# A recurrent state kernel with a feed-forward stage: all chunks read in 1,280-byte runs, state products in 64x64 quarters, weights loaded by casting transfers

## The chip, the core and the metric

The kernel runs on one core of a Trainium2 chip. The core has a matrix engine (TensorE, PE in the profile, with its weight loads listed as PEld), three elementwise engines (VectorE as DVE, ScalarE as ACT, GpSimd as POOL), a sequencer that mostly issues transfers (SyncE, SP), and 16 DMA engines. The engines run side by side and wait for each other through semaphores. The metric is the device time of one execution in microseconds, as the median of several runs.

## The reference

There are 4 batches of 8 heads, so 32 independent recurrences, over 768 steps with 40 features. Each keeps a 40 x 40 state. The output of all heads, put side by side (320 features for each of 3,072 tokens), goes through a feed-forward stage.

```
state = 0                                   # per batch and head, 40 x 40
for t in range(768):
    y[t]  = r[t] @ state
    Sa    = state @ a[t]
    state = state * w[t][None, :] - outer(Sa, b[t]) + outer(v[t], k[t])
x = y, heads side by side                   # 3072 x 320
out = square(max(x @ w_in, 0)) @ w_out      # w_in 320 x 2048, w_out 2048 x 320
```

All inputs and the output are float32 in HBM.

## The kernel before

**Chunks.** The 768 steps are cut into 12 chunks of 64. Inside a chunk the recurrence is written as matrix products; only the state passes from chunk to chunk. For each chunk the kernel takes the logarithm of w (`ln`), splits it into two bfloat16 parts (`hi`, `lo`), and sums them over the steps with triangular matmuls: `cf` gives the sums turned (features by steps), `ci` gives them straight (steps by features). Their exponentials scale a and r (decay up to a step) and k and b (its inverse).

**Turning.** The products need some operands turned, which TensorE does as transpositions: `TA`, `TR` (a and r), `TK` (k and b), `BK` (k and b turned, scaled and turned back), `TV` (v and the corrections), `TS` (the state), `XT` (the output). Each writes PSUM, and an elementwise engine copies or multiplies it out under the same name in small letters (`tA`, `tR`, `tK`, `bK`, `tV`, `tS`, `xt`). Chunks in `WHOLE` (0 to 3, function `tmode`) turn 128 x 128 at a time; later ones turn two halves of 64 rows each. A few turns go by DMA (`dK`, `dV`, `dS`).

**The products of a chunk**, for all 32 heads:
- `EN`, `CX`: the triangular matrices within the chunk, masked on DVE (`mEN`, `mCX`).
- `AS`: a against the old state; `EV`: the triangular matrix against v; `u0`, `NU`, `u1`: one correction step. Together they give the rows that update the state.
- `SC`, `S`, `s`: the new state (old state carried over, plus k and b against v and the corrections; then scaled and stored by DVE at line 808).
- `RS`, `Y`, `y`, `yd`: the output from the old state and from within the chunk.
- `F`, `FL`, `f`, `q`, `O`, `o`, `st`: the feed-forward stage of the chunk's 256 tokens: input matmuls (`F` over 256 features, `FL` over the last 64), max with 0, square, output matmuls, copy and store.

**Loading.** `load(c)` issues the six inputs of a chunk from SP, two transfers each. Where rows go by steps, a run is one head's 40 features, 160 bytes; where a partition holds eight steps, a run is 8 x 40 x 4 = 1,280 bytes. a and r use the 1,280-byte form in every chunk; k and b use it in chunks in `RUNS` (0 to 2; `turned_kb`, line 501), and the 160-byte form otherwise; w and v use 160 bytes. k and b of chunks outside `RUNS` are scaled straight (`mulKB`) and then turned. The weights come from SP as float32 into buffers used later for other things (lines 1040, 1048, 1062) and are cast by an elementwise engine (`cwl`, `cwi`, `cwo`).

**What sets the order.** The kernel lists every operation once with its reads and writes (`plan.add`), and the text `ORDER` says in which order and on which engine each is issued; `PE0` to `PE3` name the PSUM slot that a group takes. A slot is free again when the engine that empties it is done. Each engine executes its own list strictly in order, so an instruction that waits holds everything behind it on that engine. Matmuls are issued at line 402, half-row transpositions at 406 and 128 x 128 ones at 409. `rows(g)` is the lower or upper half of the 128 partitions.

**Tile shapes.** `pe(name, mode, ...)` names the array shape of a group: D is the whole 128 x 128 array, R two row halves, C two column halves, Q quarters of 64 x 64. In the kernel before, AS, RS, SC, S and Y are C; EV is C in chunks 3 to 11, for which the unused half of VU is zeroed (`zu`); NU is Q.

Of the kernel before, what the change touches and what calls it, by code (L numbers as in the profile page):

```python
# [86 lines left out]
ORDER = """SP ldw 0; SP ldb 0; SP ldk 0; POOL zv 1; POOL zr 0; SP ldk 1; ACT ln 0; SP ldb 1; POOL hi 0; ACT  # L87
castB 0; POOL zr 1; DVE lo 0; SP ldw 1; DVE castK 0; PE0 cf 0; DVE zs 0; PE1 TK 0; DVE zk 0; ACT
eg 0; SP lda 0; PE2 ci 0; POOL castB 1; DVE tK 0 g0; SP ldr 0; DVE zv 0; DVE castK 1; SP ldv 0;
ACT ln 1; ACT hi 1; POOL castA 0; ACT ef 0; SP lda 1; DVE lo 1; PE3 TA 0; ACT exw 0; DVE tK 0 g1;  # L90
SP ldw 2; PE0 cf 1; DVE tA 0 g0; ACT ef 1; DVE tA 0 g1; PE1 EN 0 g0; POOL castV 0 g1; PE2 TK 1;
DVE zk 2; SP ldb 2; ACT eg 1; DVE mEN 0 g0; POOL castV 0 g0; PE3 BK 0; POOL castA 1; SP ldk 2; DVE
tK 1 g0; POOL castR 0; POOL zv 2; DVE tK 1 g1; SP lda 2; PE1 EN 0 g1; POOL zk 1; PE0 ci 1; DVE mEN
0 g1; PE2 TA 1; ACT exw 1; SP ldr 1; ACT ln 2; DVE bK 0; PE0 EV 0; SP ldv 1; POOL castB 2; PE1 BK
1; DVE hi 2; ACT u0 0; DVE tA 1 g1; POOL lo 2; DVE bK 1; PE3 EN 1 g1; PE NU 0; DVE tA 1 g0; POOL
zs 1; ACT u1 0 g0; SP lwi 0 k1 x1; DVE mEN 1 g1; PE1 EN 1 g0; ACT u1 0 g1; PE2 S 0 g0; SP lwi 0 k1
x2; DVE mEN 1 g0; SP ldw 3; ACT castK 2; POOL castA 2; PE3 TR 0; PE S 0 g1; ACT tRw 0; PE0 cf 2;
DVE s 0 q1; PE1 TV 0; ACT eg 2; POOL castV 1 g1; DVE s 0 q0; SP lwi 0 k1 x3; PE3 ci 2; SP lwi 0 k1
x0; DVE tV 0; POOL zu 3 g0; ACT ef 2; SP lwo 0 x0; PE2 TA 2; POOL castV 1 g0; ACT exw 2; SP lwi 0
k0 x2; DVE tA 2 g1; PE0 CX 0 g0; POOL zu 3 g1; PE1 AS 1; ACT castR 1; SP lwi 0 k0 x1; DVE mCX 0  # L100
g0; PE EV 1; SP lwi 0 k0 x0; SP ldv 2; DVE tA 2 g0; PE0 CX 0 g1; ACT u0 1; PE3 TK 2; DVE mCX 0 g1;
ACT ln 3; PE NU 1; PE2 TR 1; ACT hi 3; POOL cwi 0 k1h0; DVE tK 2 g1; PE0 TS 0; ACT u1 1 g0; SP lwi
0 k0 x3; POOL cwi 0 k1h1; DVE tK 2 g0; ACT u1 1 g1; SP lwl 0; ACT tRw 1; POOL lo 3; PE1 Y 0; SP
ldb 3; PE3 EN 2 g1; ACT tS 0; DVE yd 0; DVE y 0; PE2 TV 1; POOL cwo 0 x0; DVE mEN 2 g1; PE1 SC 1;
ACT tV 1; PE S 1 g0; PE S 1 g1; PE0 EN 2 g0; DVE s 1 q0; PE3 XT 0; POOL castV 2 g0; DVE s 1 q1;
ACT xt 0; PE2 BK 2; SP ldr 2; DVE mEN 2 g0; POOL cwi 0 k0h0; ACT castV 2 g1; PE3 ci 3 h0; PE1 AS
2; POOL cwi 0 k0h1; ACT ei 3 h0; DVE bK 2; PE EV 2; ACT ex 3 h0 g1; PE0 ci 3 h1; ACT ex 3 h0 g0;
DVE u0 2; PE2 CX 1 g0; ACT ex 3 h1 g1; PE3 F 0 u0; SP lda 3; ACT ei 3 h1; DVE cwl 0; ACT ex 3 h1
g0; DVE mCX 1 g0; PE NU 2; PE0 F 0 u2; ACT u1 2 g0; SP lwo 0 x1; SP ldk 3; ACT u1 2 g1; PE2 CX 1
g1; PE FL 0 u2; DVE mCX 1 g1; PE FL 0 u0; PE1 FL 0 u1; ACT f 0 u0; PE F 0 u1; DVE f 0 u2; PE2 RS  # L110
1; ACT f 0 u1; PE3 SC 2; PE S 2 g0; POOL castA 3; PE S 2 g1; ACT q 0 u1; SP lwo 0 x2; PE0 FL 0 u3;
DVE s 2 q0; PE Y 1; DVE s 2 q1; PE1 cf 3; SP ldv 3; PE F 0 u3; ACT ef 3; DVE cwo 0 x1; DVE yd 1;
DVE y 1; PE3 TA 3; ACT f 0 u3; PE1 TV 2; DVE tA 3 g0; POOL mulKB 3 h1; ACT castR 2; SP lwo 0 x3;
DVE tA 3 g1; PE0 XT 1; PE2 TS 1; ACT xt 1; DVE mulKB 3 h0; PE3 TR 2; ACT tV 2; DVE tS 1; SP ldw 4;
PE0 TK 3; DVE cwo 0 x2; PE2 F 1 u2; DVE tK 3; ACT tRw 2; POOL castV 3 g1; PE1 FL 1 u1; PE FL 1 u2;
SP ldr 3; PE3 EN 3 g1; POOL castV 3 g0; ACT f 1 u2; PE0 EN 3 g0; DVE mEN 3 g1; PE F 1 u1; POOL cwo
0 x3; SP lwo 0 x4; PE2 F 1 u0; SP ldk 4; DVE mEN 3 g0; ACT f 1 u1; PE3 CX 2 g1; PE FL 1 u0; DVE
mCX 2 g1; PE1 CX 2 g0; ACT ln 4; PE0 TS 2; ACT f 1 u0; POOL hi 4; DVE mCX 2 g0; PE3 AS 3; POOL lo
4; PE EV 3; SP lwo 0 x5; PE2 RS 2; DVE tS 2; ACT u0 3; PE Y 2; POOL zu 4 g0; ACT castR 3; PE NU 3;
DVE y 2; PE0 FL 1 u3; ACT u1 3 g0; DVE yd 2; PE1 ci 4 h1; SP ldb 4; DVE cwo 0 x4; PE F 1 u3; ACT  # L120
ex 4 h1 g0; DVE q 0 u0; ACT u1 3 g1; DVE q 0 u2; PE2 TR 3; ACT ei 4 h1; PE3 SC 3; PE S 3 g0; ACT
# [6 lines left out]
ACT ln 5; PE3 FL 2 u3; SP ldr 5; PE F 2 u3; ACT o 0; DVE hi 5; DVE mEN 4 g0; ACT f 2 u0; POOL lo
5; PE2 RS 3; PE Y 3; SP ldw 6; ACT f 2 u3; PE0 FL 2 u1; DVE y 3; POOL q 1 u0; PE1 cf 5; DVE yd 3;
PE3 EN 4 g1; ACT ef 5; PE F 2 u1; DVE mEN 4 g1; SP lda 5; ACT castV 4 g0; PE2 XT 3; POOL castR 4;  # L130
PE1 F 2 u2; DVE xt 3; ACT castV 4 g1; POOL q 1 u3; DVE f 2 u1; SP ldb 5; PE FL 2 u2; PE2 ci 5 h0;
PE3 AS 4; ACT ex 5 h0 g1; DVE f 2 u2; PE EV 4; ACT ei 5 h0; POOL q 2 u3; PE0 TS 3; ACT ex 5 h0 g0;
DVE u0 4; ACT ln 6; PE2 ci 5 h1; SP ldk 5; PE1 TR 4; DVE tS 3; ACT ei 5 h1; POOL castR 5; PE NU 4;
# [18 lines left out]
DVE mCX 5 g1; POOL q 3 u3; ACT castV 6 g1; PE0 AS 6; SP ldr 6; PE2 RS 5; ACT f 4 u1; PE EV 6; POOL
mulKB 7 h1; PE Y 5; ACT u0 6; SP ldk 8; PE1 cf 7; DVE y 5; PE3 ci 7 h0; PE NU 6; DVE yd 5; POOL
castA 7; ACT ei 7 h0; PE2 O 3 u0; DVE u1 6 g0; ACT ln 8; SP ldr 7; ACT ef 7; DVE u1 6 g1; POOL
castR 6; PE O 3 u1; SP ldw 9; DVE hi 8; ACT ex 7 h0 g0; ACT ex 7 h0 g1; DVE q 3 u2; PE1 TA 7; PE0
TV 6; DVE mulKB 7 h0; PE3 TR 6; ACT tV 6; PE O 3 u2; DVE tA 7 g1; DVE lo 8; PE O 3 u3; SP ldv 7;
DVE tA 7 g0; ACT tR 6 g1; ACT tR 6 g0; PE0 TK 7; ACT o 3; PE1 XT 5; DVE tK 7; PE3 SC 6; PE S 6 g0;
# [966 lines left out]
```

## Time and profile before

| | |
|---|---|
| runs | 244.72 us median of 3 (241.68, 244.72, 244.88) |
| profiled execution | span 241.4 us from first to last instruction; the page gives no other time of it. The lowest run is 0.3 us above the span |
| TensorE | 219.8 us busy (91%), 5,360 matmuls |
| VectorE, ScalarE, GpSimd | 185.1 (77%), 171.9 (71%), 119.3 us (49%) |
| DMA | 116,808 packets, 37.20 MB, mean 154 GB/s; 103,575 packets under 512 bytes; the SP queue's packets take 75.7% of the 16 engines' span |
| mean granted TensorE clock | 0.975 of full speed |

A busy share is an average over stages with different limits, so it has to be read stage by stage. The timeline gives the start and the length of a group of matmuls; since matmuls overlap in the pipeline, the cost of a group in a full stretch is the start of the next group minus its own. An entry `[2.78 <-DMA raw_kb<-in_b_dram]` says that the engine sat idle 2.78 us before the instruction and that a transfer ended the wait.

### The profile page before, as it was taken

How to read it: one execution, taken by the hardware profiler on the slowest of the kernel's cores; microseconds unless marked ns; L12 is line 12 of the kernel's file. 1: busy time of each engine (PE TensorE's matmuls, PEld its weight loads, DVE VectorE, ACT ScalarE, POOL GpSimd, SP SyncE). 2: the span in 40 equal slices, each digit the busy share in tenths (PEclk: the TensorE clock that was granted, in tenths of full speed). 3: DMA queues.
4: the chain of work that ended last, by engine and by line, in shares of the span. 5: the costliest groups of instructions: out<-in, count | busy, mean ns of one | idle time of the engine just before them, and what ended most of it. 6: DMA issues, size and time to landing. Idle time of an engine off the chain costs nothing.

```text
span 241.4 us, 11825 instructions
## 1 busy us (share of the span) xinstructions
PE 219.8 (91%) x5360; PEld 173.8 (72%) x5360; DVE 185.1 (77%) x237; ACT 171.9 (71%) x225; POOL 119.3 (49%) x117
## 2 busy tenths in 40 slices
PE   0569877999999999999999999999999999999992
PEld 0357666778887787777777877877787777877872
DVE  3779994889988898899789978779888668646430
ACT  3383876879699888976979995975897974572330
POOL 6237816403545572849948379318591750024330
PEclk9967997999999999999999999999999999999998
DMA  6989999997979987888783878978994857093413
GB/s 154 233 185 231 186 217 162 187 203 156 181 158 236 187 163 148 144 194 152 157 169 67 168 178 161 220 157 144 146 188 120 156 106 93 3 161 72 109 24 86
DMA packets 116808, 37.20 MB, mean 154 GB/s; under 512 B 103575, under 2 KB 116375, under 8 KB 116503
## 3 DMA queue, kind: packets, MB, share of 16 engines
q1 hardware_dynamic: 115574, 36.13, 75.7%
q8 instruction: 42, 0.69, 1.2%
q10 hardware_dynamic: 1184, 0.33, 0.6%
q14 instruction: 8, 0.06, 0.1%
HBM read 28.84 MB, written 3.93 MB: 136 GB/s over the span
## 4 chain that ended last, share of the span: by engine, by line
PE 74%; DMA 8%; SPq 7%; DVE 4%; ACT 3%; issue 2%; POOL 1%; POOLq 0%; ACTq 0%
PE pb L402 65%; PE pb L406 6%; DMA G<-in_moe_w_in_dram 4%; PE pb L409 3%; DMA osb<-in_moe_w_out_dram 2%; SPq L433 2%; SPq L1048 2%; DMA raw_w<-in_w_dram 2%; SPq L425 1%; DVE AR L682 1%; POOL WIN L392 1%; SPq L465 1%; DVE VU L385 1%; ACT lnW L548 1%; ACT VU L388 1%
## 5 line engine op out<-in xcount | busy, mean ns | idle before, releaser
L402 PE MATMUL pb<-WOUT,G 128*128 128x320 bf16 (+1 forms) x400 | 57.0, 294 | 0.1
L973 POOL TENSOR_TENSOR G<-G 128x1024 bf16<-128x1024 bf16 x22 | 41.8, 1910 | 28.4 <-ACT G L965 23.4
L402 PE MATMUL pb<-XT,WIN 128*128 128x256 bf16 x384 | 48.3, 273 | 0.0
L402 PEld LDWEIGHTS <-G 128*128 128x128 bf16 x400 | 36.4, 98 | 13.8 <-issue 0.5
L965 ACT ACTIVATE G<-pb 128x1024 bf16<-128x1024 f32 x36 | 36.0, 1021 | 11.1 <-PE pb L402 9.6
L402 PEld LDWEIGHTS <-WIN 128*128 128x128 bf16 x384 | 34.7, 98 | 8.0 <-issue 3.7
L713 DVE TENSOR_TENSOR EN<-pb,MSK 128x1024 bf16<-128x1024 f32 x24 | 28.8, 1216 | 4.9 <-PE pb L402 4.8
L713 DVE TENSOR_TENSOR CX<-pb,MSKI 128x1024 bf16<-128x1024 f32 x24 | 28.7, 1218 | 3.5 <-PE pb L402 3.2
L396 POOL TENSOR_TENSOR KB<-raw_kb,iG 128x640 bf16<-128x640 f32 x10 | 15.8, 1580 | 16.7 <-ACT iG L584 14.9
L808 DVE TENSOR_TENSOR STb<-pb,GT 64x640 bf16<-64x640 f32 x22 | 18.1, 821 | 3.4 <-PE pb L402 3.0
L392 POOL CAST VU<-raw_v 64x640 bf16<-64x640 f32 x17 | 13.3, 785 | 13.3 <-DMA raw_v<-in_v_dram 12.8
L896 DVE TENSOR_TENSOR Yb<-pb,Gin 128x128 bf16<-128x128 f32 (+1 forms) x24 | 12.3, 553 | 9.5 <-PE pb L402 9.4
L590 ACT ACTIVATE Gin<-pb 64x320 f32<-64x320 f32 x36 | 15.4, 428 | 4.6 <-PE pb L402 4.2
L396 POOL TENSOR_TENSOR lo<-lnW,hi 128x640 bf16<-128x640 f32 x7 | 9.8, 1402 | 16.4 <-DVE hi L383 16.2
L402 PE MATMUL pb<-XT,WLAST 64*128 64x256 bf16 x192 | 17.1, 271 | 0.0
L682 DVE TENSOR_TENSOR AR<-pb,GT 128x512 bf16<-128x512 bf16 x24 | 15.9, 683 | 1.6 <-PE pb L406 1.4
L402 PEld LDWEIGHTS <-EN 64*64 64x64 bf16 (+1 forms) x768 | 14.5, 111 | 3.4 <-issue 2.2
L388 ACT ACTIVATE VU<-pb 64x640 bf16<-64x640 f32 x17 | 11.8, 697 | 7.1 <-PE pb L402 4.0
L967 DVE TENSOR_SCALAR G<-pb 128x1024 bf16<-128x1024 f32 x12 | 14.4, 1212 | 1.8 <-PE pb L402 1.8
L388 ACT ACTIVATE VUT<-pb 128x2048 bf16<-128x2048 bf16 x6 | 11.3, 1876 | 5.4 <-PE pb L406 3.1
L402 PE MATMUL pb<-UTI,hi 64*128 64x64 bf16 x192 | 8.2, 198 | 7.3 <-POOL hi L392 6.9
L584 ACT ACTIVATE iG<-pb 128x640 f32<-128x640 f32 x18 | 12.6, 700 | 2.7 <-PE pb L402 2.1
(117 smaller groups left out, 442.7 us busy)
## 6 DMA issues: line engine op xcount, KB each, us to landing
raw_kb<-in_b_dram SPq DMA_DIRECT2D x24, 160.0 KB
raw_kb<-in_k_dram SPq DMA_DIRECT2D x24, 160.0 KB
raw_a<-in_a_dram SPq DMA_DIRECT2D x24, 160.0 KB
raw_v<-in_v_dram SPq DMA_DIRECT2D x24, 160.0 KB
raw_w<-in_w_dram SPq DMA_DIRECT2D x23, 160.0 KB
...
```

What stands on the lines that cost most here:

```text
L388: alts.append(("ACT", c_act(n), lambda: nc.scalar.activation(out=o_(), in_=i_(), func=ACTF.Copy, scale=1.0 if scale is None else scale)))
L392: lambda: nc.gpsimd.tensor_copy(out=o_(), in_=i_())))
L396: return [("POOL", 40 + 2.35 * n, lambda: nc.gpsimd.tensor_tensor(out=o_(), in0=a_(), in1=b_(), op=op)), ("DVE", c_dve(n), lambda: nc.vect ...
L402: return lambda: nc.tensor.matmul(out=o_(), lhsT=l_(), rhs=r_(), start=start, stop=stop, skip_group_check=True)
L406: return lambda: nc.tensor.transpose(out=o_(), in_=i_(), identity=IDb[rows(g), :])
L590: nc.scalar.activation(out=Gin[c % NGI][rows(g), NP * jh:NP * jh + NP, :].rearrange("p j e -> p (j e)"), in_=slot(hb, FP32)[rows(g), g, 0: ...
L682: ew(f"tA {c} g{g}", [("DVE", c_dve(512), lambda g=g: nc.vector.tensor_tensor(out=steps(AR[q2][:, 0, g]), in0=turned(ha, g), in1=steps(GT[ ...
L713: evac(f"m{nm} {c} g{g}", lambda s, n: [("DVE", c_dve(n), lambda: nc.vector.tensor_tensor(out=dst[q2][:, g, s].rearrange("p q i t -> p (q ...
L808: ew(f"s {c} q{q}", [("DVE", c_dve(2 * n), lambda q=q: nc.vector.tensor_tensor(out=STb[q2][rows(q), :, q, 0:D], in0=slot(hs, FP32)[rows(q) ...
L965: ("ACT", c_act(1024), lambda gb=gb, hf=hf: nc.scalar.activation(out=gb, in_=slot(hf, FP32)[:], func=ACTF.Relu)),
L967: ("DVE", c_dve(1024), lambda gb=gb, hf=hf: nc.vector.tensor_scalar(out=gb, in0=slot(hf, FP32)[:], scalar1=0.0, scalar2=None, op0=ALU.max))],
L973: ("POOL", 1900, lambda gv=gv: nc.gpsimd.tensor_tensor(out=gv, in0=gv, in1=gv, op=ALU.mult)),
```

## The change

1. `RUNS` is all 12 chunks. k and b of every chunk come in 1,280-byte runs, are cast, turned (`TK`), scaled while leaving PSUM (`tK`, DVE, with the turned inverse `iGT`), and turned back (`BK`, `bK`). `mulKB`, `ci`, `ei` and `ex` go; `ce` sums the steps before a step, and `eg` exponentiates. The cast of a gets a buffer of its own (`tAr`). r is no longer shifted by one step, so line 1069's row of zeros goes and each chunk stores 64 rows.
2. The state lies in both partition halves (`STb`, `Sb`: 8 x 2 x 64 instead of 16 x 2 x 64 with zeros). AS and RS become 32 products each on 64 x 64 quarters instead of 16 on column halves; EV is Q in all chunks; `zu` goes. `u0` is three operations, `u1` four. `s` is one operation on 128 partitions instead of two on 64. `TS` turns half as much. S uses 40 instead of 64 weight columns after chunk 0.
3. No turn is 128 x 128 any more (`WHOLE` goes); `dK` goes.
4. The weights go from HBM straight into their bfloat16 places by 18 casting transfers issued from GpSimd; the casts go.
5. Seven fillers `WD2` of two 128 x 512 matmuls on `ones` stand in the first part of TensorE's list. `ORDER` is new throughout.

The diff, cut (lines of the new kernel stand 3 to 70 lines elsewhere):

```diff
-    WHOLE = range(4)
-    RUNS = range(3)
-    DTK, DTV, DTS = range(11, 12), range(9, 12), range(8, 11)
-    EVC = range(3, 12)
+    RUNS = range(12)
+    DTK, DTV, DTS = range(max(11, 12), 12), range(9, 12), range(8, 11)
...
-    STb = buf("STb", [128, NJ, 2, 64], BF16, 2)
-    Sb = buf("Sb", [128, NJ, 2, 64], BF16, 2)
+    STb = buf("STb", [128, NP, 2, 64], BF16, 2)
+    Sb = buf("Sb", [128, NP, 2, 64], BF16, 2)
...
+        hk = ("A", "BK", c)
+        ms = [tp(lambda p=p, x=x: slot(hk, BF16)[:, x, 64 * p:64 * p + 64],
+                 lambda p=p, x=x: KBT[q2][rows(x), p].rearrange("p y t -> p (y t)"), x)
+              for p in range(NJ) for x in range(2)]
+        pe(f"BK {c}", "R", 64, ms, reads=both(("KBT", q2)), writes=[hk], alloc=[hk])
...
-            for p in range(NP):
-                for g in range(2):
-                    ms.append(mm(uo(p, g, 0, 2), lambda p=p, g=g: AR[q2][:, 0, g, p, :],
-                                 lambda p=p, g=g: STb[(c - 1) % 2][:, NP * g + p, :, 0:D],
-                                 p % 4 == 0, False))
-            pe(f"AS {c}", "C", 80, ms, reads=[("AR", q2, 0), ("AR", q2, 1), ("STb", (c - 1) % 2, 0),
-                                             ("STb", (c - 1) % 2, 1)],
+        ALL = [(i, s, x) for i in range(NP) for s in range(2) for x in range(2)]
+            ms = [mm(uo(s, x, i), lambda i=i, s=s, x=x: AT[q2][rows(x), pair_of(s, i), :],
+                     lambda i=i, s=s, x=x: STb[(c - 1) % 2][rows(x), 4 * s + i % 4, i // 4, 0:D],
+                     i == 0, False) for i, s, x in ALL]
+            pe(f"AS {c}", "Q", 40, ms, reads=both(("AT", q2)) + [("STb", (c - 1) % 2)],
...
-            pe(f"RS {c}", "C", 80, ms, reads=[("RR", q2, 0), ("RR", q2, 1), ("Sb", (c - 1) % 2)],
+            ms = [mm(yo(s, y, i), lambda i=i, s=s, y=y: RT[q2][rows(y), s, i, :],
+                     lambda i=i, s=s, y=y: Sb[(c - 1) % 2][rows(y), 4 * s + i // 2, i % 2, 0:D],
+                     i == 0, False) for i, s, y in ALL]
+            pe(f"RS {c}", "Q", 40, ms, reads=[("RT", q2, 0), ("RT", q2, 1), ("Sb", (c - 1) % 2)],
...
-                plan.add(f"lwi 0 k{k2} x{x}", [("SP", 800)], ("ew", {"SP": lambda k2=k2, x=x:
-                         nc.sync.dma_start(out=Gf[1 - k2][32 * x:32 * x + 32],
-                                           in_=wi[k2][32 * x:32 * x + 32])}),
+                plan.add(f"lwi 0 k{k2} x{x}", [("POOL", 550)], ("ew", {"POOL": lambda k2=k2, x=x:
+                         nc.gpsimd.dma_start(out=WIN[:, k2, 512 * x:512 * x + 512],
+                                             in_=wi[k2][x])}),
...
-            plan.add(f"lwo 0 x{x}", [("SP", 1100)], ("ew", {"SP": lambda x=x:
-                     nc.sync.dma_start(out=osb[x % 2][:], in_=wo[x // 2][x % 2])}),
+            plan.add(f"lwo 0 x{x}", [("POOL", 720)], ("ew", {"POOL": lambda x=x:
+                     nc.gpsimd.dma_start(out=WOUT[:, 2 * x:2 * x + 2, :], in_=wo[x])}),
```

The start of the new order by engine, as far as the prediction speaks of it (up to `F 0 u0` on TensorE):

```
SP    w0 a0 k0 b0 w1 k1 w2 a1 b2 v0 b1 k2 r0 v1 a2 w3 a3 v2 r1 w4 r2 k3 b3 b4 k4 a4 r3 v3 ...
POOL  zk 0; castK 0; zv 0; lo 1; castA 1; castK 1; castV 0 g0; hi 2; castA 3; lwi k1 x1; castV 1 g0;
      lwl; castV 1 g1; lwi k1 x3; k0 x0; k1 x0; k0 x1; k0 x3; k1 x2; k0 x2; castR 1; hi 3; lo 3;
      lwo x4; x3; x0; x2; x1; zs 1; lwo x5; x7; castV 2 g0; lwo x6; hi 4 ...
DVE   ... mEN 0 g1; tK 1 g1; tK 1 g0; u0 0 s1; tA 1 g0; tA 1 g1; za 0; lo 2; mEN 1 g0; u1 0 x1s0;
      u1 0 x1s1; mEN 1 g1; s 0; castA 2; tR 0 g1; tR 0 g0; mCX 0 g1; mCX 0 g0; zr 1; tK 2 g1; tK 2 g0;
      tA 2 g0; tA 2 g1; yd 0; y 0; mCX 1 g1; xt 0; s 1 ...
PE    ce 0; TA 0; cf 0; TK 0; WD2; EN 0; cf 1; WD2; EN 0; ce 1; TK 1; WD2; WD2; TA 1; EV 0; BK 0; WD2;
      NU 0; EN 1; cf 2; EN 1; TV 0; S 0; TR 0; BK 1; AS 1; ce 2; CX 0; EV 1; CX 0; WD2; TK 2; NU 1;
      TA 2; WD2; TR 1; TV 1; SC 1; Y 0; BK 2; CX 1; XT 0; TS 0; S 1; cf 3; CX 1; EN 2; F 0 u0 ...
```

In the order before, SP's list begins w0 b0 k0 k1 b1 w1 a0 r0 v0 a1 w2 b2 k2 a2 r1 v1, then two pieces of w_in, w3, and further weights between the loads of chunks 2 and 3.

More of the change, by code (lines that the diff above doesn't have):

```diff
@@ L86 @@
 O_AFTER = 0
[L87 to L121, printed above, removed]
@@ L128 @@
[L128 to L133, printed above, removed]
@@ L152 @@
[L152 to L157, printed above, removed]
@@ L627, in prep @@
[L627 to L636 removed]
+                lambda s=s: iGc[:].rearrange("p (x e) (b m) -> p b x m e", x=2, b=2)[:, s], 640),
@@ L1060, in weights @@
[L1060 to L1070 removed]
+                nc.gpsimd.dma_start(out=WLAST[rows(rg)], in_=wl[rg])
```

1016 lines of the change are left out of this document (497 added, 519 removed).

## The prediction

> **What bounds the kernel now.** I read the page first (busy shares, DMA strip, chain), then busy time by stretches of 10 us, then TensorE's timeline, which gives what a group costs by when the next one starts.
>
> ```profile
> span 241.4 us, 11825 instructions
> ...
> PE 219.8 (91%) x5360; PEld 173.8 (72%) x5360; DVE 185.1 (77%) x237; ACT 171.9 (71%) x225; POOL 119.3 (49%) x117
> ...
> PE 74%; DMA 8%; SPq 7%; DVE 4%; ACT 3%; issue 2%; POOL 1%; POOLq 0%; ACTq 0%
> ```
>
> ```profile
> 0.00:10.00 10.00, 2.50 (x68) 2.15 (x70) 4.66 (x17) 3.78 (x4) 4.75 (x20) 1.00 0.77 188
> 10.00:20.00 10.00, 6.29 (x128) 5.10 (x126) 8.20 (x11) 4.92 (x6) 4.38 (x7) 0.71 0.91 190
> 20.00:30.00 10.00, 8.94 (x232) 7.15 (x232) 9.65 (x12) 7.04 (x9) 7.83 (x9) 0.95 0.93 216
> 30.00:40.00 10.00, 7.04 (x227) 6.41 (x227) 7.48 (x10) 6.95 (x10) 5.02 (x6) 0.91 1.06 205
> 40.00:50.00 10.00, 9.20 (x227) 7.44 (x226) 7.26 (x9) 7.70 (x11) 2.89 (x4) 0.92 0.88 165
> ...
> 100.00:110.00 10.00, 10.00 (x273) 7.60 (x274) 9.12 (x13) 7.30 (x12) 6.40 (x6) 1.00 0.78 169
> ```
>
> Columns: stretch, length, busy time of PE, PEld, DVE, ACT, POOL, then TensorE's granted clock, DMA share, GB/s. There are two regimes. Until about 46 us TensorE is idle a third of the time: DMA is full (0.91 to 1.06) and DVE nearly so (9.65 of 10). From there on TensorE is full (10.00 of 10) at full clock. The border is the first feed-forward group, `F 0 u0`:
>
> ```profile
> 46.42 1.05 PE L402 MATMUL pb<-XT,WIN 128*128 128x256 bf16 x8
> ```
>
> The last matmul ends, by the chain:
>
> ```profile
> 237.04 0.02 issue
> ```
>
> From `F 0 u0` to the last matmul lie 237.04 - 46.42 = 190.6 us of nearly gapless TensorE, and 241.4 - 237.0 = 4.4 us of copy and store behind it. So time = start of `F 0 u0` + TensorE work from there + 4.4. A relieved DMA or elementwise engine is worth something only in the first term; every added matmul counts in full in the second.
>
> **TensorE's work behind F 0 u0.** The price of a group, from starts in a full stretch:
>
> ```profile
> 105.65 0.48 PE L402 MATMUL pb<-STb,AR 128*64 128x80 bf16 x16
> 105.96 0.66 PE L402 MATMUL pb<-VU,EN 128*64 128x40 bf16 x32
> 106.47 0.46 PE L402 MATMUL pb<-Sb,AR 128*64 128x80 bf16 x16
> 106.75 0.66 PE L402 MATMUL pb<-KB,CX 128*64 128x40 bf16 x32
> 107.35 0.41 PE L406 MATMUL pb<-IDb,tA 64*128 64x64 bf16 x16
> 107.69 0.68 PE L402 MATMUL pb<-NZ,EN 64*64 64x40 bf16 x32
> 108.30 0.99 PE L402 MATMUL pb<-WOUT,G 128*128 128x320 bf16 x6
> ```
>
> ```profile
> 124.68 0.41 PE L406 MATMUL pb<-IDb,tA 64*128 64x64 bf16 x16
> 124.93 0.63 PE L406 MATMUL pb<-IDb,VU 64*128 64x64 bf16 x32
> 125.39 0.40 PE L406 MATMUL pb<-IDb,tR 64*128 64x64 bf16 x16
> ```
>
> ```profile
> 70.59 1.05 PE L409 MATMUL pb<-IDQ,VU 128*128 128x128 bf16 x16
> 71.64 0.57 PE L402 MATMUL pb<-WOUT,G 128*128 128x320 bf16 x3
> ```
>
> AS costs 105.96 - 105.65 = 0.31, EV 0.51, RS 0.28. A half-row transposition group costs 0.25 per 16 and 0.46 per 32 (124.68, 124.93, 125.39) when the next group has the same tile shape; before another shape the same 16 took 0.34 (107.35 to 107.69). A change of shape therefore costs 0.09. Sixteen full 128x128 transpositions cost 1.05, about 0.066 each. NU, 32 products on 64x64 quarters, takes 107.69 to 108.30 = 0.61, of which 0.09 is the change of shape: 0.52, so quarters run at EV's rate, 16 ns each.
>
> The order lists give the groups that come after `F 0 u0`:
> - AS: 9 groups x 0.31 = 2.8; after, 10 groups of 32 quarter products x 0.51 = 5.1: +2.3.
> - RS: 11 x 0.28 = 3.1; after, 11 x 0.51 = 5.6: +2.5.
> - EV: one group more behind the border: +0.5.
> - BK: none before; chunks 3 to 11 now turn k and b back, 9 x 0.46: +4.1. TK stays: 7 groups of 32 and one of 16 full ones (4.3) against 9 of 32 (4.1): -0.2.
> - TS: 48 full + 4 x 32 half = 3.2 + 1.8 = 5.0; after, 7 groups of 16 half x 0.25 = 1.8: -3.2.
> - TV: 32 full + 5 x 32 = 4.4; after, 7 x 32 = 3.2: -1.2. TA, TR and XT: 42 full ones go (-2.8), 84 half ones come (+1.3): -1.5.
> - One cumulative-sum group fewer (cf 3 is ahead of the border), ce for ci: -0.2.
> - Changes of tile shape: 150 before, 184 after (counted in the orders): 34 x 0.09 = +3.1.
>
> Sum **+6.2**. Two terms are open. S uses 40 weight columns instead of 64 from chunk 1 on: between nothing (I take it, the S group keeps 32 products of 40 columns) and, at most, the weights' share 24/64 of 9 x 0.5 = -1.7. And four quarters may run abreast where NU's two do now: a rival below.
>
> **The elementwise engines.** From the groups view:
>
> ```profile
> L808 DVE TENSOR_TENSOR STb<-pb,GT 64x640 bf16<-64x640 f32 x22 | 18.1, 821 | 3.4 <-PE pb L402 3.0
> L398 DVE TENSOR_TENSOR KB<-raw_kb,iG 128x640 bf16<-128x640 f32 x8 | 6.6, 833 | 0.8 <-DMA raw_kb<-in_b_dram 0.8
> L383 DVE COPY KBT<-pb 128x2048 bf16<-128x2048 bf16 x5 | 6.1, 1221 | 0.5 <-PE pb L406 0.5
> L528 DVE TENSOR_TENSOR KBT<-pb,iG 128x1024 bf16<-128x1024 bf16 x6 | 7.1, 1215 | 0.3 <-ACT iG L504 0.3
> L388 ACT ACTIVATE VUT<-pb 128x2048 bf16<-128x2048 bf16 x6 | 11.3, 1876 | 5.4 <-PE pb L406 3.1 <-PE pb L409 2.3
> L713 DVE TENSOR_TENSOR EN<-pb,MSK 128x1024 bf16<-128x1024 f32 x24 | 28.8, 1216 | 4.9 <-PE pb L402 4.8
> L682 DVE TENSOR_TENSOR AR<-pb,GT 128x512 bf16<-128x512 bf16 x24 | 15.9, 683 | 1.6 <-PE pb L406 1.4
> L388 ACT ACTIVATE AR<-pb 128x512 bf16<-128x512 bf16 x14 | 7.7, 593 | 2.4 <-PE pb L406 1.9 <-DVE AR L383 0.4
> ```
>
> DVE gets 18 more KBT products (+21.9) and loses 5 KBT copies (-6.1), 8 KB products (-6.6) and 11 STb products (-9.0): about 0; split u0 and u1, casts and bK copies move some 5 to 10 us onto it and onto ACT, each. Neither passes TensorE's 91%. I add 0 for it and keep 0 to +5 of new TensorE stalls for the range.
>
> **The start of F 0 u0.** DMA feeds chunk 0 and 1 in order of issue:
>
> ```profile
> 5.30 0.74 ACT L548 ACTIVATE lnW<-raw_w 128x640 f32<-128x640 f32 x1 [3.21 <-DMA raw_w<-in_w_dram]
> 9.95 0.72 POOL L392 CAST tKB<-raw_kb 128x640 bf16<-128x640 f32 x1 [2.78 <-DMA raw_kb<-in_b_dram]
> 27.82 0.71 POOL L392 CAST VU<-raw_v 64x640 bf16<-64x640 f32 x1 [0.80 <-DMA raw_v<-in_v_dram]
> ```
>
> Four loads in 1,280-byte runs (b0, k0, k1, b1) land between 5.30 and 9.95: 1.16 each. From 9.95 to 27.82 come 7 run loads and 4 in 160-byte rows (w1, v0, w2, v1): (17.9 - 8.1) / 4 = 2.44 each. These prices, put on the new order (w0 a0 k0 b0 w1 k1 w2 a1 b2 v0 b1 k2 r0 v1 a2 w3 a3), land b1 at 5.3 + 7 x 1.16 + 3 x 2.44 = 20.7 instead of 9.95, and a3 at 30.2. Chunks 0 to 2 were read in such runs already, so the start saves nothing there; the packets saved belong to chunks 3 to 11, where TensorE waits for no transfer. Chunk 1's TK cannot start before b1's cast, near 21.6; DVE then has tK 1 to s 1 in its queue, which holds the slot for `F 0 u0`: tK 1's first product begins at 22.2, and 4 KBT and 5 mask products at 1.22, 6 of 512 columns at 0.68 and an estimated 6.4 of smaller ones (two STb among them) make 21.5: 43.7 at the earliest, with no gap.
>
> GpSimd is the later path. Its queue is castA 3 (a3: 30.2 + 0.75 = 31), a weight transfer, castV 1, the two of WLAST, castV 1, seven more of WIN, castR 1. What issuing a casting transfer costs on GpSimd no row shows; nearest are SP's issues:
>
> ```profile
> 31.59 0.42 SPq L1062 DMA_DIRECT2D osb<-in_moe_w_out_dram  x1
> ...
> 34.94 6.48 SPq L1048 DMA_DIRECT2D G<-in_moe_w_in_dram  x1
> ```
>
> 0.42 free, up to 6.48 held up. I take 0.7, an estimate nearer to the free one: 31 + 3 x 0.75 + 10 x 0.7 = 40.2 for castR 1, then TR 1 (0.3), two tR (1.2), tV 1 on ACT (1.88), CX 1 (0.3), its mask (1.22), s 1 (0.82) and an estimated 1.5 us for XT's copy and the handovers: **47.5**. At 0.42 it is 44.7. Behind castR 1 stand hi 3, lo 3, seven transfers of WOUT and castV 2, which EV 2 needs: 40.2 + 2.8 + 4.9 = 48, and TensorE has some 4 us of F, RS, Y and EN ahead of EV 2.
>
> At nothing I cost: the 14 fillers (WD2), since TensorE idles for 16 us before 50 (without that cover they would cost up to 3.7 us, by 1.05 for 8 products of 256 columns at 46.42); GpSimd's and DVE's dropped weight casts, the dropped zeroing of VU and the dropped DMA transposition of KBT, which TensorE does not wait for behind the border.
>
> **Forecast.** 47.5 + 190.6 + 6.2 + 4.4 = 248.7 us of span, +7.3 on 241.4. The median of the runs, 244.72, lies 3.3 above the profiled span (lowest 241.68, about the span itself); the same 7.3 on it gives **252**.
>
> **Rivals.**
> 1. *Quarters run four abreast* (ends on the other side). Today's NU uses two of the four; if the other two work beside them, a group of 32 falls from 0.51 to 0.26: 41 groups (AS 10, EV 10, NU 10, RS 11) x 0.25 = -10.3. For it: neighbouring products fall into different row and column halves. Against: column halves (EV), row halves (transpositions) and quarters all show about 15 ns per product, as if the stream of instructions set it. Span 238.4 with F 0 at 47.5, 235.6 with F 0 at 44.7: 239 to 242 with the 3.3. It decides once a group of 32 costs less than 0.33, where 41 x 0.18 eats the 7.3. The Trainium skill, TensorEngine Tiling (Array Packing), Key Properties, says tiles load and multiply independently and lists four tiles of 64x64: by that rule the sum is this rival's.
> 2. *GpSimd's issues clog.* At 1.65 an issue, the geometric middle of SP's two rows, castR 1 comes at 31 + 2.25 + 16.5 = 50 and F 0 at 57: 258 of span, 262 with the 3.3. Each tenth of a microsecond of issue is 1 us of start. The Trainium skill, SBUF — State Buffer, "A bandwidth-pool intuition that's wrong", says a GpSimd transfer of 620 ns takes 3100 beside a VectorE copy that locks the shared port. By that rule it would be this rival if DVE were in such copies. Between 31 and 45 us DVE has one, castA 2; the rest read PSUM or two tensors.
> 3. *The start gains.* Transfers land earlier than my prices, F 0 at DVE's floor near 42 to 44: 244 to 246 of span, 247 to 249: within 2%.
> 4. *The transfers do not get cheaper.* The runs' effect on DMA fails: that changes nothing behind F 0, where nothing waits for it.
>
> **How the numbers follow.** Forecast as worked out (246 to 257) 0.53; rival 1 0.18; rival 2 0.12; rival 3 (and 4) 0.17. Two per cent, about what a measurement of this kernel tells from no change, ends at 249.6. Slower: rival 2 and most of the forecast, 0.12 + 0.47. Faster, below 239.8: half of rival 1 and a little of rival 3, 0.11. Within: the other half, the rest of rivals 3 and 4, the forecast's lower edge, 0.30. The range 241 to 259 leaves out rival 1's lower half and rival 2's end.
>
> **What would show it.** In the new profile: AS and RS groups of 32 at about 0.50 between starts (0.26 proves rival 1); `F 0 u0` near 47.5; the DMA share lower from 60 us on with no gain from it; TensorE full from F 0 to the last matmul over about 197 us; a b1 cast near 21. I am wrong if TensorE behind F 0 needs under 192 us, or if it stalls by more than 5 us for DVE or ACT.

## Result and the profile after

The changed kernel takes 254.56 us (median of four runs, 252.46 to 256.80) against 243.81 for the kernel before: a ratio of **1.0415, 95% interval 1.0326 to 1.0505**, slower by about 4%. The forecast was 252. The number was close partly by luck, since errors of opposite sign partly cancel in it. The start is 7.0 us later than forecast. The work behind it is 2.6 us shorter, which is itself the sum of two larger misses: the products on quarters are some 9 us cheaper, and waits and a half clock that were put at nothing cost some 7. Executions come in a fast and a slow state; the ratios compare fast ones alone, and of the traces below only that of more_fill is of a slow one.

The page after, in the lines that answer to those of before:

```profile
span 252.4 us, 13429 instructions
...
PE 221.4 (88%) x6198; PEld 168.0 (67%) x6198; DVE 190.1 (75%) x258; ACT 175.8 (70%) x237; POOL 84.5 (33%) x96
...
q8 instruction: 48, 0.79, 1.3%
...
PE 58%; DVE 10%; SPq 8%; ACT 7%; issue 7%; DMA 4%; POOL 4%; POOLq 0%; DVEq 0%; ACTq 0%
```

TensorE carries 58% of the chain instead of 74%, and "issue", time in which TensorE waited for nothing that the profile shows, 7% instead of 2%. Busy time by stretches (columns as in the prediction):

```profile
20.00:30.00 10.00, 6.47 (x205) 4.19 (x203) 6.86 (x10) 7.36 (x13) 2.10 (x3) 1.00 0.84 186
30.00:40.00 10.00, 7.87 (x245) 5.79 (x245) 7.04 (x10) 8.37 (x10) 8.67 (x14) 0.58 1.11 188
40.00:50.00 10.00, 8.01 (x256) 6.21 (x255) 6.17 (x8) 6.52 (x10) 8.94 (x12) 0.67 1.18 266
50.00:60.00 10.00, 5.66 (x155) 4.43 (x155) 3.18 (x3) 5.14 (x7) 0.71 (x1) 0.67 1.15 188
60.00:70.00 10.00, 9.96 (x240) 7.35 (x237) 7.39 (x11) 5.68 (x11) 2.12 (x3) 0.71 0.31 72
...
100.00:110.00 10.00, 10.00 (x297) 7.32 (x295) 8.73 (x14) 9.91 (x14) 2.82 (x4) 1.00 0.44 101
```

Later the DMA share is lower (0.44 instead of 0.78 from 100 to 110), and nothing comes of it, as forecast. New is what stands between 30 and 70: a granted clock of 0.58 to 0.71, and from 50 to 60 every engine but the DMAs half idle. TensorE's timeline there, in its waits named "issue" and the first feed-forward group (`F 0 u0`):

```profile
40.04 0.74 PE L409 MATMUL pb<-IDb,tKB 64*128 64x64 bf16 x21 [0.75 <-issue]
...
46.25 0.62 PE L405 MATMUL pb<-KB,CX 128*64 128x40 bf16 x27 [1.08 <-issue]
...
52.45 0.32 PE L405 MATMUL pb<-VU,KB 128*40 128x40 bf16 x7 [2.51 <-issue]
...
54.52 0.82 PE L405 MATMUL pb<-XT,WIN 128*128 128x256 bf16 x3
...
59.19 0.94 PE L405 MATMUL pb<-KB,CX 128*64 128x40 bf16 x27 [1.89 <-issue]
```

And the end of the chain of waits:

```profile
234.16 14.53 PE pb L405 x140
...
248.71 0.44 ACT osb L391
```

So the span is 54.5 (start of `F 0 u0`) + 194.2 (to the end of TensorE's last matmul, 248.7) + 3.7. Forecast was 47.5 + 196.8 + 4.4; before had 46.4 + 190.6 + 4.4.

### The profile page after: what moved, and what is told of

It reads as the page before. It is cut to its first block, busy times and chain, and to the rows that moved or that the text cites. A ratio compares the mean times of both kernels' runs of the same rounds, so it can differ in the third digit from the quotient of the medians.

```text
span 252.4 us, 13429 instructions
## 1 busy us (share of the span) xinstructions
PE 221.4 (88%) x6198; PEld 168.0 (67%) x6198; DVE 190.1 (75%) x258; ACT 175.8 (70%) x237; POOL 84.5 (33%) x96
## 2 busy tenths in 40 slices
DMA packets 80567, 33.36 MB, mean 132 GB/s; under 512 B 61568, under 2 KB 80512, under 8 KB 80512
## 4 chain that ended last, share of the span: by engine, by line
PE 58%; DVE 10%; SPq 8%; ACT 7%; issue 7%; DMA 4%; POOL 4%; POOLq 0%; DVEq 0%; ACTq 0%
PE pb L405 47%; PE pb L409 9%; SPq L435 5%; DVE EN L716 2%; POOL G L923 2%; DVE CX L716 2%; DMA raw_kb<-in_k_dram 2%; PE pb L1015 2%; SPq L430 1%; DVE KBT L608 1%; SPq L424 1%; DMA raw_r<-in_r_dram 1%; DMA raw_kb<-in_b_dram 1%; ACT VU L391 1%; ACT KB L391 1%
## 5 line engine op out<-in xcount | busy, mean ns | idle before, releaser
L915 ACT ACTIVATE G<-pb 128x1024 bf16<-128x1024 f32 x41 | 41.6, 1020 | 13.5 <-PE pb L405 13.2
L923 POOL TENSOR_TENSOR G<-G 128x1024 bf16<-128x1024 bf16 x16 | 30.6, 1922 | 30.6 <-ACT G L915 26.3
L608 DVE TENSOR_TENSOR KBT<-pb,iGT 128x1024 bf16<-128x1024 bf16 x24 | 28.4, 1217 | 5.3 <-PE pb L409 2.5
L716 DVE TENSOR_TENSOR CX<-pb,MSK 128x1024 bf16<-128x1024 f32 x24 | 28.9, 1220 | 4.5 <-PE pb L405 4.1
L581 ACT ACTIVATE iGT<-pb 128x1024 f32<-128x1024 f32 x12 | 12.3, 1023 | 13.8 <-PE pb L405 13.7
L925 ACT ACTIVATE G<-G 128x1024 bf16<-128x1024 bf16 x19 | 19.8, 1050 | 0.1
L855 DVE TENSOR_TENSOR Yb<-pb,Gex 128x128 bf16<-128x128 f32 (+1 forms) x24 | 12.3, 551 | 9.2 <-PE pb L405 9.1
L391 ACT ACTIVATE VU<-pb 64x320 bf16<-64x320 f32 x34 | 14.6, 430 | 4.1 <-DVE VU L388 2.0
L631 DVE TENSOR_TENSOR AT<-pb,GT 128x512 bf16<-128x512 bf16 x24 | 15.6, 681 | 1.2 <-ACT GT L578 0.6
L405 PE MATMUL pb<-AT,KBT 64*128 64x64 bf16 x384 | 10.2, 198 | 3.6 <-DVE KBT L608 2.8
L578 ACT ACTIVATE GT<-pb 128x1024 f32<-128x1024 f32 x12 | 12.2, 1020 | 1.5 <-DVE STb L789 1.3
L391 ACT ACTIVATE osb<-pb 128x640 f32<-128x640 f32 (+1 forms) x9 | 6.0, 670 | 10.3 <-PE pb L405 10.3
```

What stands on the lines that cost most here:

```text
L391: alts.append(("ACT", c_act(n), lambda: nc.scalar.activation(out=o_(), in_=i_(), func=ACTF.Copy, scale=1.0 if scale is None else scale)))
L405: return lambda: nc.tensor.matmul(out=o_(), lhsT=l_(), rhs=r_(), start=start, stop=stop, skip_group_check=True)
L581: ew(f"ef {c} i", [("ACT", c_act(1024), lambda: nc.scalar.activation(out=iGT[0][:].rearrange("p (g m) t -> p g m t", g=2), in_=sums_t(), f ...
L608: ew(f"tK {c} g{g}", [("DVE", c_dve(1024), lambda g=g, gm=gm: nc.vector.tensor_tensor(out=KBT[q2][:, gm].rearrange("p m x (k i) -> p x m k ...
L631: ew(f"tA {c} g{g}", [("DVE", c_dve(512), lambda g=g: nc.vector.tensor_tensor(out=AT[q2][:, NP * g:NP * g + NP].rearrange("p m (k i) -> p ...
L716: ew(f"m{nm} {c} g{s}", [("DVE", c_dve(1024), lambda: nc.vector.tensor_tensor(out=dst[q2][:, s].rearrange("p q i t -> p (q i) t"), in0=slo ...
```

## The experiments

**What was to be told apart.** Behind `F 0 u0`, whether four quarters run side by side (rival 1). Ahead of it, what makes the start late: theory A, TensorE's own instruction list, which comes in pieces through the DMA queue `q8` (48 packets for 6,198 matmuls and as many weight loads: 129 matmuls a packet) and comes late while weights and inputs fill the DMAs; theory B, the halved clock; theory C, the order of the loads and casts. In the table, "piece" is the last wait named "issue" ahead of `F 0 u0`, at the time it ends.

| kernel | piece | F 0 u0 | span | ratio to before (95%) |
|---|---|---|---|---|
| changed kernel | 52.45 | 54.52 | 252.4 | 1.0415 (1.0326–1.0505) |
| late_wout | 50.75 | 52.83 | 249.5 | 1.0422 (1.0331–1.0514) |
| no_fill | 50.81 | 52.47 | 254.2 | 1.0489 (1.0361–1.0616) |
| two_quarters | 51.17 | 53.24 | 253.7 | 1.0567 (1.0482–1.0652) |
| more_fill | 52.23 | 54.44 | 256.2 | 1.0479 (1.0368–1.0590) |
| tiny_fill | 56.20 | 58.28 | 255.8 | 1.0546 (1.0459–1.0633) |
| b1_early | 51.33 | 53.41 | 251.9 | 1.0490 (1.0400–1.0579) |
| calm | 50.66 | 52.66 | 249.4 | 1.0405 (1.0311–1.0499) |
| improved | 49.51 | 51.02 | 248.1 | 1.0344 (1.0262–1.0425) |
| before_tiny | 43.06 | 45.06 | 239.9 | 1.0017 (0.9963–1.0071) |
| whole_only | 51.16 | 51.61 | 253.3 | 1.0537 (1.0462–1.0611) |
| whole_start | 50.34 | 50.59 | 256.7 | 1.0717 (1.0634–1.0800) |
| aligned | 47.71 | 48.95 | 249.0 | 1.0371 (1.0314–1.0428) |

**two_quarters**, the order of the products in AS, EV, NU and RS.

```diff
-        ALL = [(i, s, x) for i in range(NP) for s in range(2) for x in range(2)]
+        ALL = [(i, s, s ^ d) for d in range(2) for i in range(NP) for s in range(2)]
```

> The changed kernel with the 32 products of AS, EV, NU and RS in another order: first those of one diagonal pair of quarters, then those of the other, instead of all four in turn. Theory A (four quarters run side by side, two at most do so in the new order): a group of 32 goes from 0.27 (105.19 to 105.47 us in the changed kernel) to about 0.52, which with 41 groups is +10, span 262 and time 263 to 265. Theory B (the groups are short for another reason, such as 40 columns or half the rows): 0.27 stays, time within 1.5 of 254.6.

In the changed kernel's timeline a group of AS costs 105.47 - 105.19 = 0.28 before another group on quarters, and one of RS 98.11 - 97.75 = 0.36 before another tile shape:

```profile
97.75 0.44 PE L405 MATMUL pb<-Sb,RT 64*64 64x40 bf16 x32
98.11 0.69 PE L405 MATMUL pb<-KB,CX 128*64 128x40 bf16 x32
...
105.19 0.44 PE L405 MATMUL pb<-STb,AT 64*64 64x40 bf16 x32
105.47 0.45 PE L405 MATMUL pb<-VU,EN 64*64 64x40 bf16 x32
105.85 0.41 PE L409 MATMUL pb<-IDb,STb 64*128 64x64 bf16 x16
```

In two_quarters the same places of its timeline read:

```profile
96.62 0.58 PE L405 MATMUL pb<-Sb,RT 64*64 64x40 bf16 x32
97.14 0.69 PE L405 MATMUL pb<-KB,CX 128*64 128x40 bf16 x32
...
104.22 0.49 PE L405 MATMUL pb<-STb,AT 64*64 64x40 bf16 x26
104.53 0.21 PE L405 MATMUL pb<-VU,EN 64*64 64x40 bf16 x2
104.55 0.19 PE L405 MATMUL pb<-STb,AT 64*64 64x40 bf16 x2
...
105.05 0.41 PE L409 MATMUL pb<-IDb,STb 64*128 64x64 bf16 x16
```

RS goes from 0.36 to 0.52, AS and EV together from 0.66 to 0.83. Both expectations missed: the groups did not stay short, and the span rose by 1.3, not by 10 (by 2.6 behind `F 0 u0`, which came 1.3 earlier in this trace). The 0.28 of the changed kernel is about half of the 0.52 that NU's 32 products of the same shape cost on two quarters in the kernel before. So the products do run four abreast in the changed kernel, and the order decides how well; but RS costs 0.16 more, not 0.25, and AS and EV only 0.17 together. The rows at 104.53 and 104.55 suggest why the price is small: products of EV already start while some of AS, which stand ahead of them in the list, are still to come. Between products on different quarters TensorE's list is thus not executed strictly in order, as was said of every engine above. That nothing else keeps the price small is not shown.

**no_fill**: the seven fillers (`PE0 WD2` and so on) left out of the order.

> The changed kernel without its seven fillers (14 matmuls of 512 columns on ones). Instruction loading: the waits named 'issue' stand after 637, 767, 895 and 1025 matmuls, 128 to 130 apart; with 14 fewer ahead, the one that now splits S 1 after 25 of its 32 products moves 14 matmuls further down the list, into the group cf 3. If instead S 1's own operands cause it, it stays in S 1. Clock: if the fillers hold the clock up, it falls to half before 31.6 us and F 0 u0 stays within 1.5 us of 54.5 or comes later, though up to 5 us of TensorE are gone; if they only cost, F 0 u0 starts 2 to 4 earlier and the time falls to 250 to 252.

```profile
31.97 1.04 PE L408 MATMUL pb<-IDb,KBT 64*128 64x64 bf16 x32 [0.38 <-DVE STb L788]
32.94 0.62 PE L404 MATMUL pb<-STb,AT 64*64 64x40 bf16 x32
...
48.02 0.73 PE L404 MATMUL pb<-VU,KB 128*40 128x40 bf16 x32
...
50.81 0.24 PE L404 MATMUL pb<-UTI,lo 64*128 64x64 bf16 x2 [1.79 <-issue]
```

S 1 (48.02) runs through, and the wait has moved into cf 3, as theory A says: its place is a count of matmuls, not an operand. On the clock: 32 half-row turns take 32.94 - 31.97 = 0.97 here, twice their 0.46 to 0.50 at full speed, and groups keep such prices until about 56. In the changed kernel the fillers buy full speed from 24.5 to 31.6. `F 0 u0` comes 2 us earlier without them although the clock falls, which neither expectation had, and nothing of it is left at the end (254.52 against 254.56 in the medians).

**more_fill** (`PE3 WD4` ahead of cf 2, `PE0 WD4` ahead of TR 0) does the opposite.

> The changed kernel with eight more filler matmuls of 512 columns, four ahead of cf 2 and four ahead of TR 0, where TensorE waits between 28 and 33 us. Clock theory: TensorE's idle share there (about half of 28.2 to 31.6) is what drops the granted clock to half from 31.6 to 45.3; with the fillers it stays full for at least 3.4 us more, the groups there take half their time, and F 0 u0 starts 1 to 4 us earlier, time 250 to 254. Rival: another engine or the transfers set F 0 u0 and the clock there is covered: F 0 u0 within 1 us of 54.5 or up to 1.7 later, time 254 to 257.

```profile
34.02 0.73 PE L409 MATMUL pb<-IDb,KBT 64*128 64x64 bf16 x32
...
39.40 0.59 PE L409 MATMUL pb<-IDb,tKB 64*128 64x64 bf16 x29 [1.23 <-issue]
...
45.76 0.74 PE L405 MATMUL pb<-STb,IDQ 128*64 128x320 bf16 x3 [2.63 <-issue]
...
52.23 0.46 PE L405 MATMUL pb<-VU,KB 128*40 128x40 bf16 x15 [1.86 <-issue]
```

The clock now is full from 31 to 46, and `F 0 u0` does not move: 54.44. Whatever TensorE gains it waits out at the next border: 1.23, 2.63 and 1.86 instead of 0.75, 1.08 and 2.51. The pieces come every 6.4 us (39.40, 45.76, 52.23), as in the changed kernel (40.04, 46.25, 52.45: every 6.2). So the half clock of this stretch does not set `F 0 u0`, and theory B falls for it. The eight added matmuls also moved the borders eight products up the list, to 15 left of S 1 instead of 7.

**tiny_fill** adds a whole piece (`PE3 WT128`, 128 matmuls of 8 columns) ahead of cf 2.

> The changed kernel with 128 more matmuls of 8 columns on 64x64 quarters ahead of cf 2, where TensorE waits 1.1 us (28.4 to 29.5); by 8 ns each they are 1.1 us of work. Loading theory: TensorE's list comes in pieces of 128 matmuls, and from about 34 us on a piece takes 6.2 us to come (waits at 40.04, 46.25, 52.45, 59.19); one piece more ahead of F 0 u0 moves it by 4 to 6 us, to 59 to 61, the waits stand at the same products of the list (after 21 of TK 2, inside S 1), and the time rises by 3 to 6. Rival: the operands or the clock set the start; the fillers lie in a wait, F 0 u0 stays within 1 us of 54.5 and the time within 1.5 of 254.6.

```profile
44.34 0.74 PE L409 MATMUL pb<-IDb,tKB 64*128 64x64 bf16 x21 [1.75 <-issue]
...
56.20 0.32 PE L405 MATMUL pb<-VU,KB 128*40 128x40 bf16 x7 [3.49 <-issue]
```

The waits stand at the very products where the changed kernel has them (21 of TK 2 left, 7 of S 1), one piece later, and `F 0 u0` is 3.8 us later, a little less than expected. The median rose by 1.4 us instead of 3 to 6, which the intervals do not tell from nothing.

**before_tiny** adds the same 128 to the kernel before, ahead of TA 0.

> The kernel before with 128 more matmuls of 8 columns on 64x64 quarters ahead of TA 0, where TensorE waits 2.64 us (10.8 to 13.4): 931 instead of 803 matmuls ahead of F 0 u0, nearly the changed kernel's 935. Loading theory: from about 30 us on a piece of 128 matmuls takes 5.6 us to come here (waits at 32.29 and 37.93); one piece more moves F 0 u0 from 46.4 to 50 to 52, the waits grow and come after the same products, and the time rises by 3 to 6. That alone would be most of what the changed kernel's start is later. Rival: the matmuls lie in a wait, F 0 u0 stays within 1 us and the time within 1 of the kernel before.

```profile
37.42 0.47 PE L402 MATMUL pb<-KB,CX 128*64 128x40 bf16 x19 [1.19 <-issue]
...
45.06 1.05 PE L402 MATMUL pb<-XT,WIN 128*128 128x256 bf16 x8
```

A miss: `F 0 u0` is 1.4 us earlier and the time the same, as the rival had it. So the number of matmuls ahead of a point does not by itself set its time. A reading made after the fact, and not tested, is that TensorE has idle time to spare between 10 and 20 us, so that 128 more are free there, and that theory A holds only where TensorE uses up a piece in less than the 6 us in which the next one comes. The wait at the 19 remaining products of the KB,CX group, found in the kernel before at 37.93, is at the same product, because the list has moved by exactly one piece.

**late_wout** moves the eight transfers of w_out behind `POOL hi 4`; **calm** moves also `SP ldb 4`, `ldk 4`, `lda 4` behind `SP ldv 3`.

> The changed kernel with the eight transfers of w_out issued by GpSimd behind hi 4 (57 us) instead of from 42 us on; their data is first used at 80.75 us. Theory A: TensorE's waits named 'issue' in the changed kernel (0.75 us at 40.04, 1.08 at 46.25, 2.51 at 52.45, 1.89 at 59.19) are the loading of its own next instructions, held up because weight transfers fill DMA (share 1.1 to 1.4 from 44 to 58 us). Then the waits at 52.45 and 59.19 fall below 1 us each, F 0 u0 starts near 52 instead of 54.5, the stretch at half clock from 59 to 66 goes, and the time falls by 4 to 8 to 246 to 250. Theory B: the waits have nothing to do with the transfers; they keep their length, and the time stays within 1.5 of the changed kernel's 254.6.

> The kernel with w_out issued behind hi 4 (252.8 us, F 0 u0 at 52.83, waits of 1.36 at 44.28 and 2.94 at 50.75, DMA share 1.15 from 35 to 50), in which also b, k and a of chunk 4 are loaded behind r and v of chunk 3 instead of ahead of them, about 10 us later. Loading theory: with a megabyte less between 37 and 48 us the DMA share there falls below 1, the waits at 44 and 50 shrink to 1 us or less each, F 0 u0 starts near 50 and the time is 248 to 251. Rival: the waits keep their length whatever the share; F 0 u0 within 1 us of 52.8, time within 1.5 of 252.8.

Late_wout, by stretches of 5 us, and its waits:

```profile
40.00:45.00 5.00, 3.19 (x108) 2.18 (x104) 2.86 (x5) 4.33 (x7) 3.46 (x5) 0.98 1.15 253
45.00:50.00 5.00, 2.06 (x101) 1.64 (x93) 2.55 (x4) 2.56 (x3) 0.00 (x0) 0.70 1.13 297
50.00:55.00 5.00, 4.25 (x119) 3.34 (x119) 3.18 (x3) 1.94 (x2) 0.00 (x0) 0.61 0.78 114
55.00:60.00 5.00, 4.92 (x185) 3.87 (x184) 3.90 (x7) 4.05 (x7) 4.54 (x7) 1.00 0.68 89
```

```profile
50.75 0.32 PE L405 MATMUL pb<-VU,KB 128*40 128x40 bf16 x7 [2.94 <-issue]
...
69.79 0.39 PE L409 MATMUL pb<-IDb,KBT 64*128 64x64 bf16 x15 [1.61 <-issue]
```

Where the DMAs stay full (input loads took the place of w_out up to 50) the wait of 2.94 stays; where they are calm (0.78, 0.68) the one at 59 is gone, and with it the half clock after it; and where w_out now passes, at 69.79 (DMA share 1.23 from 65 to 70), there is a new one. Calm did not do what it was to do: its DMA share from 37 to 48 stayed at 1.17. The wait ahead of S 1's end is 0.16 instead of 2.94 (share 0.86 from 46 to 50), but 2.47 stand a piece earlier (46.11), and `F 0 u0` at 52.66 and 252.04 us are what the rival expected. These rows fit waits that follow the full DMAs, but do not prove it; late_wout's expected gain is half there in the span (2.9), and neither kernel's ratio tells it from nothing.

**b1_early** loads b of chunk 1 right behind k of chunk 1.

> The changed kernel with b of chunk 1 loaded right behind k of chunk 1, four loads earlier. By the chain of waits b1's landing at 20.3 us, its cast and TK 1 (21.20, after a wait of 1.18) hold the start. If that sets F 0 u0, b1's cast comes near 14 instead of 20.4, TK 1 up to 3 us earlier, F 0 u0 2 to 3 us earlier (52) and the time 251 to 253. If instruction loading or what stands behind sets it, TK 1 is earlier and F 0 u0 stays within 1 us of 54.5.

TK 1 comes at 19.71 instead of 21.20, AS 1 at 31.5 instead of 34.7, and then:

```profile
45.13 0.62 PE L405 MATMUL pb<-KB,CX 128*64 128x40 bf16 x27 [2.54 <-issue]
...
51.33 0.33 PE L405 MATMUL pb<-VU,KB 128*40 128x40 bf16 x7 [2.52 <-issue]
```

Of the 3.2 us, 1.1 are left at `F 0 u0`, between the two expectations; the rest is waited out at the borders, and the time stays (254.49).

**improved** joins calm, b1_early and no_fill, loads r of chunk 1 ahead of w3, v2 and a3, and puts on GpSimd the casts of v1 and r1 ahead of that of a3.

> The calmer order with more: no fillers, b of chunk 1 four loads earlier, r of chunk 1 ahead of w3, v2 and a3, and on GpSimd the casts of v1 and r1 ahead of that of a3. If the start is what the changed kernel loses, each of these takes something off it: F 0 u0 at 46 to 49, time 244 to 248, level with the kernel before. If the loading of 128 matmuls per 6 us sets the start by itself, F 0 u0 stays at 50 to 52 and the time at 249 to 252.

250.65 us: the lowest here beside aligned (251.27), still 3.4% over the kernel before, and its interval overlaps with that of the changed kernel. `F 0 u0` at 51.02 and the time are what the second theory expected of it. So of theory C no more is shown than the 3.5 us by which `F 0 u0` comes earlier in this order, in which the fillers and w_out are changed too.

**whole_only** and **whole_start** turn 128 x 128 at a time again in the start, alone and on top of improved; XT stayed in halves, so 176 matmuls fewer, not 182.

```diff
+        if c in WK:
+            ms = [tpw(lambda i=i, y=y: wide_steps(hb, y)[:, :, i, :],
+                      lambda i=i, y=y: tKB[y][:, i].rearrange("p q e -> p (q e)"))
+                  for i in range(8) for y in range(2)]
```

> The changed kernel with turns of 128x128 put back in its start (TK, BK, TA in chunks 0 to 2, TR and TV in chunks 0 and 1, TS and XT in chunk 0): 753 instead of 935 matmuls ahead of F 0 u0, though each turn takes longer (16 of 128x128 1.05 us, 32 halves 0.46, at full clock). Loading theory: 182 matmuls are 1.4 pieces of 6.2 us; F 0 u0 at 46 to 50 instead of 54.5, the time 246 to 250. Rival (operands, clock or TensorE's own work set the start): some 11 turns take 0.3 to 0.6 longer, F 0 u0 at 54 to 58, time 254 to 258.

> The same turns of 128x128 put into the improved order (250.65 us, F 0 u0 at 51.02): 739 matmuls ahead of F 0 u0. If loading still sets its start, F 0 u0 comes at 44 to 47 and the time at 243 to 247, level with the kernel before or under it. If DVE and ACT (both near 5 of 5 us from 25 to 30) set it, F 0 u0 stays at 49 to 51 and the time at 249 to 251.

Both missed. `F 0 u0` comes 2.9 and 3.9 us before the changed kernel's, not 4 to 10. In whole_start that is 0.4 ahead of improved's, within what its rival (DVE and ACT set the start) expected; so there the count of matmuls does not set the start. Whole_only's time is not to be told from the changed kernel's (255.09), and whole_start is 7.8 us slower than improved. Most of this loss arises behind 110 us, where the two orders are the same. TensorE's waits behind 110 us, whole_start:

```profile
PE pb L404 <- issue: 5.6, 6, 1.5
...
PE pb L408 <- issue: 0.9, 2, 0.8
```

Columns: us in total, times, longest. The changed kernel has no wait on "issue" there at all, and improved 0.2 us. By the piece theory, fewer matmuls ahead shift all later borders onto other products.

**aligned** tests just that: whole_start and `PE2 WT62` ahead of EN 0 g0, so that the list is exactly one piece of 128 shorter than that of the changed kernel.

> The improved order with turns of 128x128 (258.4 us) and 62 matmuls of 8 columns more, ahead of EN 0 g0, where TensorE waits 4.83 us. That order has 190 matmuls fewer ahead of the main part than the changed kernel; with the 62 it has exactly 128 fewer. Piece theory: TensorE's list comes in pieces of 128 matmuls, and a piece whose border falls where TensorE uses one up faster than the next comes costs a wait; the changed kernel's order has its borders where this costs nothing behind 60 us, and 190 fewer move each border by 62 matmuls onto other products, which cost 6.5 us of 'issue' in eight waits behind 110 us. With the 62 the borders are back at the changed kernel's products: these waits go (under 1 us in all), and the time falls by 5 to 8 to 250 to 253, though the kernel does more. Rival: the waits come from the DMA load or the shorter start; then 62 matmuls more change nothing, time within 1.5 of 258.4.

```profile
PE pb L408 <- issue: 0.7, 1, 0.7
...
PE pb L404 <- issue: 0.3, 2, 0.2
```

6.5 us of waits become 1.0, and 258.4 become 251.27: 62 matmuls more make the kernel 7 us faster (the intervals of the ratios lie apart). So the piece theory holds for where the waits stand and what they cost in the main part. For the start it holds less far, as before_tiny and whole_start show.

## Why the prediction was right, and where it was wrong

- **Frame** (start of `F 0 u0` + TensorE's work + tail): its sum holds (54.5 + 194.2 + 3.7). Its use was too simple: what a kernel gains at `F 0 u0` was not kept (in its trace no_fill is 2.0 earlier there and 1.8 later at the end), since TensorE waits again behind it.
- **Groups behind F 0 u0, +6.2**: wrong in one price. "Quarters run at EV's rate, 16 ns each" rested on NU of before, which uses two of the four quarters. On all four, 32 products cost 0.28; for 41 groups that is 9.4 less than taken, and +6.2 becomes -3.2. Rival 1 had the mechanism (it took 10.3 off), though not the time, 239 to 242. Two of the other prices held: S with 40 weight columns costs 0.61 per 32 products before an `FL` group (71.11 to 71.72) against 0.60 with 64 before (51.91 to 52.51), nothing saved, as taken; a change of shape 0.36 - 0.28 = 0.08, against 0.09.
- **TensorE stalls, "0, with 0 to +5 in the range"**: the waits behind `F 0 u0` rose from 1.1 to 4.4 us (sums over the timelines), 1.9 of it "issue", the rest DVE, ACT and GpSimd in pieces of 0.2 to 0.5. Inside the range, but from a cause that I had not named. From 59 to 65.5 the clock is at half beside it, for 6.3 us of busy time some 3.2 us lost, and about 0.5 from 54.5 to 55.5. Together 190.6 - 3.2 + 3.3 + 3.7 = 194.4, against 194.2 measured.
- **Start, transfers**: right. b1's cast starts at 20.42 (forecast 20.7 for the landing), a3's at 30.34 (30.2 for the landing).
- **Start, GpSimd**: right, rival 2 is out: castR 1 is done at 39.1 (forecast 40.2). Seven issues take 3.73 us for w_in, 0.53 each; five take 3.64 for w_out, 0.73 each; I took 0.7.

```profile
30.34 0.71 POOL L395 CAST tAr<-raw_a 128x640 bf16<-128x640 f32 x1 [6.93 <-DMA raw_a<-in_a_dram]
...
34.60 3.73 POOL L991 DMA_DIRECT2D WIN<-in_moe_w_in_dram  x7
38.38 0.72 POOL L395 CAST tR<-raw_r 128x640 bf16<-128x640 f32 x1
...
42.34 3.64 POOL L996 DMA_DIRECT2D WOUT<-in_moe_w_out_dram  x5
```

- **Start, "F 0 u0 at 47.5"**: wrong by 7.0, and this is the step that failed: "then TR 1 (0.3), two tR ... and the handovers". I let TensorE be ready whenever its operands were. It was not: castR 1 is done at 39.1, but TR 1 starts at 42.89, behind TK 2, which waits for its piece until 40.04; the next pieces come at 46.25 and 52.45, and `F 0 u0` follows the last by 2.1, in six of the kernels made from this one by 2.0 to 2.2. From 39.1 to 54.5 TensorE is busy for 10.25 of 15.4 us, at a mean clock of 0.61, and waits 4.3 us for pieces; the forecast had 7.3 us for this way and counted 0.6 of TensorE's work in it (TR 1 and CX 1). Both waits of before (0.78 and 1.07) were in the trace, some 130 matmuls apart, and I had not read them as a rule.
- **Rival 3** (the start gains) is out; **rival 4** had its cause wrong and its consequence right: the packets fell from 116,808 to 80,567 and the DMA share with them, and nothing behind `F 0 u0` had waited for them.
- **Fillers at nothing**: nearly right in the end (no_fill is no faster), though `F 0 u0` would come 2 us sooner without them.

What stays open: how the later start divides between the pieces, the operands and the half clock. NU 0 is 3.5 us later than before (27.58 against 24.05), ahead of any wait for a piece, and b1_early takes 2.7 of that away without any gain at the end. No order tried brings the changed kernel level with the one before.
